# Attention projections in plain float32, one head on each half of the array's rows

## The chip, the cores and the metric

The kernel runs on one core of a Trainium2 chip. The number that counts is the device time of that core in microseconds (us), as the median over several executions. Beside the timed executions there is one profiled execution, whose trace records every instruction with its start, its duration and what it waited for. TensorE (PE) does the matrix products and the transposes, VectorE (DVE) and ScalarE (ACT) work on what PE leaves in PSUM, GpSimd (POOL) works on SBUF tiles only, and SyncE (SP) issues most transfers. PSUM has eight banks; a bank holds 512 float32 values in each of its 128 partitions.

## The reference

Attention without a softmax over the sequence (random features), and then a gated feed-forward layer without top-k or routing. B = H = 8, S = 576, D = 64, M = 128; 4608 tokens, d_model 512, d_ff 1536, all float32.

```python
def phi(x):                                   # x is q or k, scaled by 64 ** -0.25
    proj = np.einsum('bhsd,md->bhsm', x, omega)
    h = proj - np.sum(x * x, axis=-1, keepdims=True) / 2.0
    h = h - np.max(h, axis=-1, keepdims=True)
    return np.exp(h) / np.sqrt(m)

kv = np.einsum('bhsm,bhsd->bhmd', phi(k), v)
num = np.einsum('bhsm,bhmd->bhsd', phi(q), kv)
den = np.einsum('bhsm,bhm->bhs', phi(q), np.sum(phi(k), axis=2))[..., None] + 1e-06
x = num / den                                 # then all heads of a token side by side: 4608 x 512
out = (sigmoid(x @ w_gate) * (x @ w_val)) @ w_out
```

The change concerns the einsum for `proj`, for q and for k: 64 values of one head times a 64x128 matrix, for every token and head.

## The kernel before

**The stages.** A first stage, to about 531 us of the trace, does the attention and at the same time the first third of the gate and value products (`first_pass`, tile `gv`, line 246), chunk of tokens by chunk of tokens as the attention delivers them. Then the rest of the first pass is done while the last weights are converted. From 618 us on a second pass does the other products (`gated`, tile `gw`, line 350), and after it the output product (`last`, tile `po`, line 464). The last two are Strassen-like schemes in which every operand is split into a rounded part and a remainder, so that three products in the fast 32-bit type `fp32r` give float32 accuracy.

**The attention.** Two batch rows (1152 tokens, nine tiles of 128) form a unit u, of which there are four; p is a pair of heads, of which there are four; b is the half of the nine tiles that belongs to one batch row, the tile in the middle (number 4, `MID`) being shared. A task is one (u, p, b) of k or of q, or the squared norms of one (u, b). `projected` (line 508) is common to k and q. The tile `raw` holds the two heads of a pair one above the other: 64 rows of the partitions are head 0, 64 are head 1. `om_sb` has omega's transpose twice, in the upper left and the lower right block, and zeros elsewhere, so that one product with 128 rows gives 256 columns, 128 for each head.

For this product raw is split on ACT (`hi`, line 70) and POOL (`lo`, line 71), omega once in the same way, and each tile of tokens takes three `fp32r` products of 128x256 that add up (lines 546 to 548). `GROUPS` says which tiles of tokens share a bank: two tiles of both heads, that is 4 x 128 columns. DVE then takes the maximum over each 128 columns (`mx`, line 551), and joins it with the norm (`hm`, line 555).

For k (`keys`, line 560) DVE makes the bias `nb` (line 573), ACT the exponentials (line 586), one instruction for each tile and head, and PE the products with v (`pkv`, line 594), in plain float32. For q (`queries`, line 602) DVE makes `sub` (line 612) and `h` (line 614), PE transposes `h` (`pt`, line 625), ACT takes the exponential of a whole bank (`qp`, line 627), PE multiplies with kv (`pn`, line 637, plain float32), DVE divides (lines 642 to 648), PE transposes again (`px`, line 654), ACT copies (`xs`, line 660) and issues the transfer to `xT` in DRAM, from where `first_pass` loads it. The middle tile of q belongs to two batch rows: there line 637 issues two products, each with 64 of the 128 columns of the array.

**What sets the order.** Each engine works through its own list in a fixed order. The lists are made when the program is built: the generators of the tasks are advanced in turn (`attention`, up to six at a time), the attention by `RATE` steps for each half product of `first_pass`, and a scheduler then orders each engine's instructions by what is ready. Tiles come from pools with a fixed number of buffers (`RAWS`, `SPLITS`, `HS`, `XS` and so on); who wants a buffer waits until its last reader is done. Of the eight banks two belong to `gv` and six to the attention.

Of the kernel before, what the change touches and what calls it, by code (L numbers as in the profile page):

```python
# [9 lines left out]
F32 = mybir.dt.float32  # L10
# [17 lines left out]
GROUPS = {"k": (((0, 1), (2, 3), (4,)), ((5, 6), (7, 8))), "q": (((0, 1), (2, 3)), ((4,), (5, 6), (7, 8)))}  # L28
# [22 lines left out]
RATE = 14  # L51

RAWS, SPLITS, KPS, VS, HS, XS = 6, 5, 8, 3, 4, 3
# [46 lines left out]
def attn_glu_kernel(ctx: ExitStack, tc, qT, kT, qn, kn, va, om, ident, w, out):  # L100
# [411 lines left out]
    def projected(pool, name, u, p, b, src):  # L512
# [10 lines left out]

        groups = GROUPS[name][b]
        for some in (groups,) if name == "k" else [(g,) for g in groups]:
            parts = []
            for tiles in some:
                id_ = f"{name}{u}_{p}_{tiles[0]}"
                nt = len(tiles)
                hi, lo = (  # L530
                    pool.tile([P, 2 * P], F32R, tag=tag, bufs=SPLITS, name=f"{tag}{id_}")[:, : nt * P]
                    for tag in ("hi", "lo")
                )
                o = (tiles[0] - t0) * P
                split(nc, hi, lo, raw[:, o : o + nt * P], lo_engine=nc.gpsimd)
                parts.append((id_, tiles, hi, lo))
            yield None
            i0, i1 = some[0][0] - t0, some[-1][-1] + 1 - t0
            mx = pool.tile([P, MID + 1, 2], F32, tag="mx", bufs=4, name=f"mx{id_}")
            pps = []  # L540
            for id_, tiles, hi, lo in parts:
                pp = any_bank(f"pp{id_}")[:, : len(tiles) * 2 * M]
                for i, t in enumerate(tiles):
                    c = slice(i * P, (i + 1) * P)
                    o = pp[:, i * 2 * M : (i + 1) * 2 * M]
                    nc.tensor.matmul(o, lhsT=lo[:, c], rhs=omH, start=True, stop=False)
                    nc.tensor.matmul(o, lhsT=hi[:, c], rhs=omL, start=False, stop=False)
                    nc.tensor.matmul(o, lhsT=hi[:, c], rhs=omH, start=False, stop=True)
                pp = pp.rearrange("p (i m) -> p i m", m=M)
                m = mx[:, tiles[0] - t0 : tiles[-1] + 1 - t0]  # L550
                nc.vector.tensor_reduce(out=m.rearrange("p t h -> p (t h)"), in_=pp, axis=AX.X, op=ALU.max)  # L551
                pps.append((id_, tiles, pp))
# [7 lines left out]
    def keys(pool, u, p, b):  # L560
        kp = {}
        if b:
            kp[MID] = kmid.pop((u, p))
# [313 lines left out]
```

## Time and profile before

| | |
|---|---|
| median of 3 runs | 1262.45 us (1262.18 to 1266.67) |
| profiled execution, first to last instruction | 1265.4 us |
| mean granted TensorE clock in it | 0.954 |
| busy: PE, DVE, ACT, POOL | 1186.0, 876.1, 529.0, 542.9 us |
| attention (first transfer to last transpose) | 0 to about 531 us |
| rest of the first pass | 531 to 618 us |
| second pass and output product | 618 to 1265 us |

The page counts a matmul as busy from its start to the modelled end of its pipeline, so that matmuls overlap in the records: what one costs in a dense stretch is the distance from its start to the next one's. A plain float32 matmul stands in the trace as two records, each with a weight load of its own; an `fp32r` matmul and a transpose stand there as one. The row and column PEclk give the share of the full TensorE clock that was granted.

### The profile page before, as it was taken

The numbers are of one execution on the slowest core, as the hardware profiler recorded it, in microseconds if no ns is written. First come the engines' busy times: TensorE is split into PE (matmuls) and PEld (weight loads), VectorE is DVE, ScalarE is ACT, GpSimd is POOL, SyncE is SP. The second block draws the span as 40 slices with busy tenths as digits, with TensorE's granted clock in tenths as the row PEclk, the third lists the DMA queues.
The fourth block names the chain that finished last, engine by engine and source line by source line (L and its number), as shares of the span: only waits on it lengthen the run. The fifth ranks groups of instructions, "written<-read, shape, count | busy, mean of one in ns | idle before, by whom it ended". The sixth has DMA issues, their size and how long they took to land.

```text
span 1265.4 us, 23998 instructions
## 1 busy us (share of the span) xinstructions
PE 1186.0 (94%) x8828; PEld 1122.2 (89%) x8828; DVE 876.1 (69%) x1907; ACT 529.0 (42%) x1164; POOL 542.9 (43%) x599
## 2 busy tenths in 40 slices
PE   5789989999998999987999999999999899999998
PEld 5789878788977988865999999999998899999998
DVE  4788877999777565564666565665667777777773
ACT  5456755656344544322522222323234444343331
POOL 2454334755456232144176666666666311111110
PEclk7689879999889999998999999999999999999999
DMA  7557767776555331176423333233328676666662
GB/s 244 191 179 237 219 209 243 254 253 230 183 203 174 124 122 38 60 267 223 166 88 121 139 132 109 102 121 122 130 88 285 208 218 194 206 194 183 185 198 93
DMA packets 104950, 219.43 MB, mean 173 GB/s; under 512 B 11136, under 2 KB 42112, under 8 KB 103040
## 3 DMA queue, kind: packets, MB, share of 16 engines
q1 hardware_dynamic: 87984, 198.94, 47.5%
q10 hardware_dynamic: 16848, 18.95, 4.3%
q8 instruction: 70, 1.15, 0.4%
q14 instruction: 48, 0.39, 0.1%
HBM read 141.82 MB, written 76.02 MB: 172 GB/s over the span
## 4 chain that ended last, share of the span: by engine, by line
PE 66%; DVE 13%; DMA 7%; issue 6%; POOL 4%; ACT 2%; SPq 1%; ACTq 0%; DVEq 0%; POOLq 0%
PE gw L350 25%; PE po L464 20%; PE gv L246 6%; PE pkv L594 4%; PE pnq L637 4%; PE ptq L625 2%; DMA xT<-xsq 2%; DVE mxq L551 1%; DVE hq L614 1%; DMA u<-w 1%; DVE mxk L551 1%; DMA natk<-kn 1%; DVE hmq L555 1%; DMA rawk<-kT 1%; DVE u L215 1%
## 5 line engine op out<-in xcount | busy, mean ns | idle before, releaser
L350 PE MATMUL gw<-xl,u 128*128 128x256 f32 x3024 | 362.3, 282 | 4.2 <-DVE u L330 3.5
L350 PEld LDWEIGHTS gw<-xl,u 128*128 128x128 f32 x3024 | 361.1, 189 | 5.4 <-DVE u L330 4.3
L464 PE MATMUL po<-u,yh 128*128 128x256 f32 x1512 | 272.4, 283 | 0.0
L464 PEld LDWEIGHTS po<-u,yh 128*128 128x128 f32 x1512 | 234.7, 191 | 0.0
L464 PE MATMUL po<-u,yl 128*128 128x256 f32 x756 | 214.0, 283 | 4.0 <-DVE yl L71 4.0
L246 PE MATMUL gv<-xe,wh 128*128 128x512 f32 (+1 forms) x640 | 206.3, 397 | 1.6 <-POOL xe L71 1.4
L70 ACT ACTIVATE yh<-yr 128x896 fp32r<-128x896 f32 x108 | 100.2, 950 | 158.2 <-PE po L464 86.9
L464 PEld LDWEIGHTS po<-u,yl 128*128 128x128 f32 x756 | 144.2, 191 | 4.4 <-DVE yl L71 4.4
L246 PE MATMUL gv<-xe,wl 128*128 128x512 f32 (+1 forms) x320 | 128.1, 403 | 14.1 <-DVE ye L274 7.9
L246 PEld LDWEIGHTS gv<-xe,wh 128*128 128x128 f32 x640 | 119.6, 199 | 19.1 <-POOL xe L71 3.3
L71 POOL TENSOR_TENSOR yl<-yr,yh 128x896 fp32r<-128x896 f32 x17 | 37.9, 2228 | 216.0 <-PE po L464 139.9
L71 DVE TENSOR_TENSOR yl<-yr,yh 128x896 fp32r<-128x896 f32 x91 | 103.0, 1144 | 31.3 <-PE po L464 18.3
L330 DVE TENSOR_TENSOR u<-gw,p 128x256 f32<-128x256 f32 x144 | 60.7, 421 | 58.9 <-PE gw L350 50.5
L594 PEld LDWEIGHTS pkv<-v,kpk 128*128 128x128 f32 x512 | 82.3, 220 | 21.5 <-ACT kpk L586 18.5
L594 PE MATMUL pkv<-v,kpk 128*128 128x66 f32 x512 | 88.3, 301 | 12.9 <-ACT kpk L586 12.5
L71 POOL TENSOR_TENSOR lok<-rawk,hik 128x256 fp32r<-128x256 f32 (+1 forms) x80 | 54.4, 697 | 98.6 <-ACT hik L70 98.4
L71 POOL TENSOR_TENSOR loq<-rawq,hiq 128x256 fp32r<-128x256 f32 (+1 forms) x80 | 57.5, 727 | 81.0 <-ACT hiq L70 77.6
L246 PEld LDWEIGHTS gv<-xe,wl 128*128 128x128 f32 x320 | 63.3, 199 | 24.9 <-DVE ye L274 9.1
L455 DVE TENSOR_TENSOR yr<-yr 128x128 f32<-128x128 f32 x144 | 58.2, 437 | 38.9 <-DMA yr<-ye 38.4
L637 PEld LDWEIGHTS pnq<-kv,qpq 128*128 128x128 f32 (+1 forms) x640 | 73.0, 195 | 4.8 <-ACT qpq L627 2.8
L637 PE MATMUL pnq<-kv,qpq 128*128 128x66 f32 (+1 forms) x640 | 76.5, 279 | 0.7 <-ACT qpq L627 0.7
L586 ACT ACTIVATE kpk<-ppk,nb 128x128 f32<-128x128 f32 x256 | 69.7, 391 | 15.9 <-DVE nb L573 15.6
(116 smaller groups left out, 2171.7 us busy)
## 6 DMA issues: line engine op xcount, KB each, us to landing
yl<-yl SPq DMA_DIRECT2D x36, 896.0 KB, 3.9
yr<-yl SPq DMA_DIRECT2D x72, 448.0 KB, 3.6
xr<-xT SPq DMA_DIRECT2D x68, 256.0 KB, 4.4
c<-w SPq DMA_DIRECT2D x22, 512.0 KB, 5.4
w<-c SPq DMA_DIRECT2D x11, 1024.0 KB, 4.7
v<-va SPq DMA_DIRECT2D x32, 330.0 KB, 3.3
natk<-kn SPq DMA_DIRECT2D x36, 256.0 KB, 4.5
natq<-qn SPq DMA_DIRECT2D x36, 256.0 KB, 3.8
```

The lines of the kernel that those rows point to most:

```text
L70: nc.scalar.activation(out=hi, in_=x, func=AF.Copy)
L71: (lo_engine or nc.vector).tensor_tensor(out=lo, in0=x, in1=hi.bitcast(F32), op=ALU.subtract)
L246: nc.tensor.matmul(gv, lhsT=u[:, s], rhs=v, start=(m == 0), stop=(m == 3 * KC - 1))
L330: return nc.vector.tensor_tensor(out=o, in0=a, in1=b, op=ALU.add)
L350: nc.tensor.matmul(o, lhsT=u[:, k, s], rhs=v[:, kc, :], start=(first and m == 0), stop=(m == 5), skip_group_check=not first,)
L455: nc.vector.tensor_tensor(out=raw[:, o], in0=raw[:, a], in1=raw[:, b], op=op)
L464: nc.tensor.matmul(o, lhsT=u[:, i, :], rhs=v[:, k, :], start=(j + m == 0 and n in (1, 6, 5, 4)), stop=(j == NPAIR - 1 and m == 2), skip_gr ...
L551: nc.vector.tensor_reduce(out=m.rearrange("p t h -> p (t h)"), in_=pp, axis=AX.X, op=ALU.max)
L586: nc.scalar.activation(out=kp[t][:, h, :], in_=pp[:, 2 * i + h, :], func=AF.Exp, bias=nb[:, t - t0, h : h + 1], scale=SCALE,)
L594: nc.tensor.matmul(pkv[:, h, :], lhsT=kp[b * MID + i][:, h, :], rhs=v[:, i, h, :], start=(i == 0), stop=(i == MID),)
L625: nc.tensor.transpose(out=pt[:, i, :], in_=h_sb[:, i, :], identity=id_sb)
L637: nc.tensor.matmul(pn[r, 2 * i + h, :], lhsT=qp[:, 2 * i + h, r], rhs=kvs[u, p, bb][:, h, :], start=True, stop=True,)
```

## The change

The projections are done in plain float32 from `raw` and `om_sb` themselves: the copies `hi` and `lo`, their pools, and the split of omega go. For a group of several tiles (`by_head`) each head has a product of its own, on its own 64 rows of the array with omega's 64x128 block, and its own bank; the products of the two heads alternate. The groups have four tiles instead of two, so that a bank again holds 4 x 128 columns, now of one head. A middle tile that stands alone (`both_heads`) is one product with all 128 rows and 256 columns, as before, but in plain float32. What follows works by bank as it did, with `mx`, `hm` and `sub` for four tiles at once, and `x`, `px`, `xs` and the transfer to `xT` too. `RATE` goes from 14 to 12 and `HS` from 4 to 5.

```diff
-GROUPS = {"k": (((0, 1), (2, 3), (4,)), ((5, 6), (7, 8))), "q": (((0, 1), (2, 3)), ((4,), (5, 6), (7, 8)))}
+GROUPS = {"k": (((0, 1, 2, 3), (4,)), ((5, 6, 7, 8),)), "q": (((0, 1, 2, 3),), ((4,), (5, 6, 7, 8)))}
...
-RATE = 14
-
-RAWS, SPLITS, KPS, VS, HS, XS = 6, 5, 8, 3, 4, 3
+RATE = 12
+
+RAWS, KPS, VS, HS, XS = 6, 8, 3, 5, 3
...
-    omH = const.tile([P, 2 * M], F32R, name="omH")
-    omL = const.tile([P, 2 * M], F32R, name="omL")
-    split(nc, omH, omL, om_sb)
...
+        def by_head(tiles):
+
+            pps = [any_bank(f"pp{name}{u}_{p}_{tiles[0]}_{h}") for h in range(2)]
+            for i, t in enumerate(tiles):
+                for h in range(2):
+                    r = slice(h * D, (h + 1) * D)
+                    nc.tensor.matmul(
+                        pps[h][:, i * M : (i + 1) * M], lhsT=raw[r, (t - t0) * P : (t - t0 + 1) * P],
+                        rhs=om_sb[r, h * M : (h + 1) * M], start=True, stop=True, skip_group_check=True,
+                    )
+            return [(tiles, (h,), pp.rearrange("p (i m) -> p i m", m=M)) for h, pp in enumerate(pps)]
+
+        def both_heads(t):
+
+            pp = any_bank(f"pp{name}{u}_{p}_{t}")[:, : 2 * M]
+            nc.tensor.matmul(pp, lhsT=raw[:, (t - t0) * P : (t - t0 + 1) * P], rhs=om_sb, start=True, stop=True)
+            return [((t,), (0, 1), pp.rearrange("p (i m) -> p i m", m=M))]
+
...
-                split(nc, hi, lo, raw[:, o : o + nt * P], lo_engine=nc.gpsimd)
...
-                    nc.tensor.matmul(o, lhsT=lo[:, c], rhs=omH, start=True, stop=False)
-                    nc.tensor.matmul(o, lhsT=hi[:, c], rhs=omL, start=False, stop=False)
-                    nc.tensor.matmul(o, lhsT=hi[:, c], rhs=omH, start=False, stop=True)
...
+            for tiles in some:
+                for part in by_head(tiles) if len(tiles) > 1 else both_heads(tiles[0]):
+                    ts, hs, pp = part
+                    m = mx[:, ts[0] - t0 : ts[-1] + 1 - t0, hs[0] : hs[-1] + 1]
+                    m = m.rearrange("p t h -> p (t h)")
+                    nc.vector.tensor_reduce(out=m, in_=pp, axis=AX.X, op=ALU.max)
+                    pps.append(part)
...
+            x = pool.tile([P, nt, 2, D], F32, tag="x", bufs=XS, name=f"x{id_}")
+            parts = []
+            for ts, hs, pp in pps:
+                n = nt * len(hs)
+                h_sb = pool.tile([P, n, M], F32, tag="h", bufs=HS, name=f"h{id_}_{hs[0]}")
...
+            for hs, n, h_sb in parts:
+                pt = any_bank(f"pt{id_}_{hs[0]}")[:, : n * P].rearrange("p (i s) -> p i s", s=P)
...
+            for hs, n, qp in qps:
+                pn = any_bank(f"pn{id_}_{hs[0]}")[:, : n * E].rearrange("p (i e) -> p i e", e=E)
```

**Where instructions now stand.** Three places on PE's list show it. In the changed program line 527 is the product of one head (64 rows), 536 that of a middle tile, 592 is `pkv`, 243 is `gv`. In a name such as `ppk_3_0_1`, 3 is the pair, 0 the first tile of the group, and the last number the head.

Before, PE's list in the second unit: the end of a k projection with its middle tile, and what follows it.

```order
L548 MATMUL ppk_2_2_1949<-omH,hik_2_2_1908 128x256
L546 MATMUL ppk_2_4_1957<-omH,lok_2_4_1913 128x256
L547 MATMUL ppk_2_4_1957<-omL,hik_2_4_1912 128x256
L548 MATMUL ppk_2_4_1957<-omH,hik_2_4_1912 128x256
L637 MATMUL pnq_1_7_1981<-kv_1_1_1047,qpq_1_7_1921 128x66 x4
```

Every projection is a triple of 128x256, and all of them use all rows and columns of the array.

The changed program, PE's list in the same unit: the middle of a k projection, into which another pair's `pkv` is put.

```order
L527 MATMUL ppk_3_0_0_1771<-om_sb,rawk_3_0_1710 128x128
L592 MATMUL pkv_2_0_1720<-v_2_0_1676,kmid_2_4_0_1690 128x66
L592 MATMUL pkv_2_0_1720<-v_2_0_1676,kp_2_0_1_1685 128x66 x4
L592 MATMUL pkv_2_0_1720<-v_2_0_1676,kmid_2_4_0_1690 128x66
L527 MATMUL ppk_3_0_1_1772<-om_sb,rawk_3_0_1710 128x128
```

Products with 64 rows now stand next to products with 128, and a pair of heads can be torn apart by other work.

The changed program, a little further on, where a q projection meets the first pass.

```order
L243 MATMUL gv_0_0_1857<-xe_3_1854,wl_238 128x512
L527 MATMUL ppq_1_0_0_1900<-om_sb,rawq_1_0_1805 128x128
L243 MATMUL gv_0_0_1857<-xe_3_1854,wh_237 128x512 x2
L527 MATMUL ppq_1_0_1_1901<-om_sb,rawq_1_0_1805 128x128
L527 MATMUL ppq_1_0_0_1900<-om_sb,rawq_1_0_1805 128x128
```

Here a single product of 64 rows stands between two of the first pass. Over the whole list the 512 products of line 527 form 86 unbroken runs, 37 of them of eight products and 18 of a single one; before, the 288 tiles of tokens took 864 products, and now they take 512 of line 527 and 32 of line 536.

More of the change, by code (lines that the diff above doesn't have):

```diff
@@ L537, in projected @@
             yield None
             i0, i1 = some[0][0] - t0, some[-1][-1] + 1 - t0
-            mx = pool.tile([P, MID + 1, 2], F32, tag="mx", bufs=4, name=f"mx{id_}")
+            mx = pool.tile([P, MID + 1, 2], F32, tag="mx", bufs=4, name=f"mx{name}{u}_{p}_{some[0][0]}")
             pps = []
[L541 to L552, printed above, removed]
+            for tiles in some:
[5 more added lines that the diff above has]
+                    pps.append(part)
@@ L553, in projected @@
             s = sq[:, i0:i1, 2 * p : 2 * p + 2]
-            hm = pool.tile([P, MID + 1, 2], F32, tag="hm", bufs=4, name=f"hm{id_}")[:, i0:i1]
+            hm = pool.tile([P, MID + 1, 2], F32, tag="hm", bufs=4, name=f"hm{name}{u}_{p}_{some[0][0]}")[:, i0:i1]
             nc.vector.scalar_tensor_tensor(
@@ L594, in keys @@
                 nc.tensor.matmul(
[L595 removed]
+                    pkv[:, h, :], lhsT=kp[b * MID + i, h], rhs=v[:, i, h, :],
                     start=(i == 0), stop=(i == MID),
@@ L622, in queries @@
-            yield
-            pt = any_bank(f"pt{id_}")[:, : n * P].rearrange("p (i s) -> p i s", s=P)
-            for i in range(n):
-                nc.tensor.transpose(out=pt[:, i, :], in_=h_sb[:, i, :], identity=id_sb)
-            qp = pool.tile([P, n, P], F32, tag="qp", bufs=HS, name=f"qp{id_}")
-            nc.scalar.activation(out=qp, in_=pt, func=AF.Exp)
-            yield
-            pn = any_bank(f"pn{id_}")[:, : n * E].rearrange("p (i e) -> p i e", e=E)
-            for i, t in enumerate(tiles):
-                if t == MID:
-                    mine = ((0, slice(0, P // 2)), (1, slice(P // 2, P)))
-                else:
-                    mine = ((b, slice(0, P)),)
-                for h in range(2):
+            x = pool.tile([P, nt, 2, D], F32, tag="x", bufs=XS, name=f"x{id_}")
@@ new lines, in queries @@
+            yield
+            qps = []
+            for hs, n, h_sb in parts:
+                pt = any_bank(f"pt{id_}_{hs[0]}")[:, : n * P].rearrange("p (i s) -> p i s", s=P)
+                for i in range(n):
+                    nc.tensor.transpose(out=pt[:, i, :], in_=h_sb[:, i, :], identity=id_sb)
+                qp = pool.tile([P, n, P], F32, tag="qp", bufs=HS, name=f"qp{id_}_{hs[0]}")
+                nc.scalar.activation(out=qp, in_=pt, func=AF.Exp)
+                qps.append((hs, n, qp))
+                yield
```

94 lines of the change are left out of this document (44 added, 50 removed).

## Prediction

> **What bounds the kernel now.** I read the windows by stage first, since the change touches the attention alone.
>
> ```profile
> core 0: us, PE busy (x) PEld busy (x) DVE busy (x) ACT busy (x) POOL busy (x), PEclk, DMA share, GB/s
> 0.00:64.00 64.00, 44.62 (x208) 42.66 (x209) 38.30 (x82) 32.33 (x90) 23.06 (x32) 0.69 0.66 218
> 64.00:192.00 128.00, 113.70 (x818) 106.88 (x816) 106.13 (x273) 78.12 (x216) 56.97 (x67) 0.86 0.67 210
> 192.00:531.00 339.00, 318.48 (x2216) 280.82 (x2217) 253.30 (x645) 170.10 (x474) 149.70 (x178) 0.97 0.52 172
> 531.00:618.00 87.00, 74.70 (x301) 59.10 (x301) 48.28 (x69) 26.16 (x40) 37.48 (x32) 0.92 0.57 201
> 618.00:1265.40 647.40, 634.53 (x5290) 632.79 (x5288) 430.06 (x842) 222.33 (x345) 275.74 (x292) 1.00 0.48 159
> ```
>
> The last 647 us are not touched by the change. In the attention, from 192 us on, PE is busy for 318 of 339 us at a clock of 0.97: what PE is spared or given there is time. Before that the clock is lower and PE waits more. DVE is full in two stretches only:
>
> ```profile
> 64.00:160.00 96.00, 87.45 (x674) 83.59 (x673) 83.30 (x216) 60.17 (x167) 45.46 (x53) 0.91 0.68 213
> 224.00:320.00 96.00, 90.88 (x632) 78.64 (x630) 90.79 (x208) 57.00 (x161) 58.58 (x67) 0.99 0.72 239
> ```
>
> That is 87% and 95%, in 192 of the attention's 531 us. Then the waits of PE up to 531 us (us in total, times, longest):
>
> ```profile
> PE pkv L594 <- ACT kpk L586: 12.5, 12, 2.8
> PE ppk L546 <- POOL lok L71: 10.3, 2, 8.8
> PE ppq L546 <- POOL loq L71: 0.9, 1, 0.9
> ```
>
> The split of q and k, for all its 112 us on POOL, makes PE wait 11.2 us, and 8.8 of these are the program's start, where the first transfer is on its way till 7.5. So the change is to be judged mainly by what the projections cost PE.
>
> **The projections on PE.** There are 144 records in each of six groups like the first and last here, 864 in all:
>
> ```profile
> L546 PE MATMUL ppk<-omH,lok 128*128 128x256 f32 x144 | 46.9, 325 | 11.2 <-POOL lok L71 10.3 <-ACT qpq L627 0.9
> ...
> L547 PE MATMUL ppq<-omL,hiq 128*128 128x256 f32 x144 | 41.9, 291 | 0.0
> ```
>
> These durations overlap; the cost is the step between starts. First and last of 18 in a row, and the next thing:
>
> ```profile
> 440.55 0.28 PE L546 MATMUL ppq<-omH,loq 128*128 128x256 f32 x1
> ...
> 442.54 0.28 PE L548 MATMUL ppq<-omH,hiq 128*128 128x256 f32 x1
> 442.66 0.27 PE L625 MATMUL ptq<-id_sb,hq 128*128 128x128 f32 x1
> ```
>
> (442.66 - 440.55) / 18 = 0.117 us, so 864 x 0.117 = 101 us at the full clock.
>
> What a plain float32 product costs is shown by `pnq`, two records each, on the whole array and, for the middle tile, on halves of its columns:
>
> ```profile
> 449.61 1.90 PE L637 MATMUL pnq<-kv,qpq 128*128 128x66 f32 x16
> 451.35 0.49 PE L654 MATMUL pxq<-id_sb,xq 128*128 128x128 f32 x3
> ...
> 246.08 0.69 PE L637 MATMUL pnq<-kv,qpq 128*64 128x66 f32 x16
> 246.70 0.39 PE L546 MATMUL ppq<-omH,loq 128*128 128x256 f32 x1
> ...
> 247.04 0.28 PE L548 MATMUL ppq<-omH,hiq 128*128 128x256 f32 x1
> 247.25 0.45 PE L637 MATMUL pnq<-kv,qpq 128*64 128x66 f32 x8
> 247.63 0.50 PE L246 MATMUL gv<-xe,wl 128*128 128x512 f32 x1
> 247.97 0.62 PE L246 MATMUL gv<-xe,wh 128*128 128x512 f32 x2
> 248.43 0.39 PE L246 MATMUL gv<-xe,wl 128*128 128x512 f32 x1
> ```
>
> On the whole array a record takes 1.74 / 16 = 0.109 us. On column halves 16 records take 0.62 and 8 take 0.38, so a further record costs (0.62 - 0.38) / 8 = 0.030: a half-sized weight load would explain 0.055, and the rest is that two halves work at once. But each such run has a price at its ends. From the `ppq` before it to the second `gv` behind it there are 247.97 - 247.04 = 0.93 us; in a dense stretch these steps would be 0.117 + 8 x 0.030 + 0.23 (0.46 for two `gv`, last rows) = 0.59. So a change between whole array and halves and back costs 0.34 us.
>
> No row shows halves of rows. Take it that they behave as halves of columns do. A record has 128 weight columns, so 0.109, and two records of different heads go together. Following PE's new list run by run, with alternating heads paired, the 512 products take 286 places of two records: 286 x 2 x 0.109 = 62 us. There are 86 runs; a run's first weight load is twice that of the rows above, 0.05 more, so 86 x 0.39 = 34 us. The 32 middle tiles are two records of 128x256: at least what fp32r takes, 0.23, at most what two fp32r records of 128x512 take, 0.46; since the column halves pass 66 columns in up to 0.06 us, which makes 0.23 for 256, I take the upper end, 15 us. Together 111 against 101: **PE is given 10 us**. The bounds: with nothing for the ends of runs -24; with no pairing and no ends 512 x 2 x 0.109 + 15 = 127, +26; with both prices +59.
>
> The Trainium skill says under "Key Properties" of "TensorEngine Tiling (Array Packing)" that tiles run independently of one another, but that a change of the tiling mode drains TensorE. The trace agrees for column halves, with the 0.34 us above; for row halves no run here shows it. "TensorE: Matmul & The Clock Gate", Part 3, "Measured speedup vs the span model", gives 3.07 for four row tiles; an estimate from that page, 1.53 for two, would put the 512 products at 112 / 1.53 = 73 us instead of 62, and the result 11 us higher.
>
> **What else goes.**
>
> ```profile
> L71 POOL TENSOR_TENSOR lok<-rawk,hik 128x256 fp32r<-128x256 f32 (+1 forms) x80 | 54.4, 697 | 98.6 <-ACT hik L70 98.4
> L71 POOL TENSOR_TENSOR loq<-rawq,hiq 128x256 fp32r<-128x256 f32 (+1 forms) x80 | 57.5, 727 | 81.0 <-ACT hiq L70 77.6 <-PE ppq L546 2.7 <-DMA rawk<-kT 0.5
> L70 ACT ACTIVATE hik<-rawk 128x256 fp32r<-128x256 f32 (+1 forms) x80 | 30.2, 392 | 20.1 <-PE ppk L548 9.2 <-PE ppq L548 8.3 <-POOL lok L71 1.5
> L555 DVE SCALAR_TENSOR_TENSOR hmq<-mxq,sqq 128x4 f32<-128x4 f32 x64 | 19.1, 312 | 0.0
> L612 DVE TENSOR_TENSOR subq<-sqq,hmq 128x4 f32<-128x4 f32 x64 | 17.6, 288 | 0.1
> L85 DVE TENSOR_SCALAR c<-c 128x512 uint32<-128x512 uint32 x22 | 13.2, 602 | 0.1
> 556.07 0.42 DVE L85 TENSOR_SCALAR late<-late 128x512 uint32<-128x512 uint32 x1
> ```
>
> PE's waits for the split: 1.3 at the start (8.8 less 7.5), 1.5 and 0.9 later, **-4** (bounds 0 and -11). On DVE 32 of the 64 `hm` and 32 of the `sub` go, 32 x (0.312 + 0.288) = 19 us; DVE sets the pace in 192 of 531 us, that is 7, and since PE is nearly full in the same stretches I count half, **-4** (0 and -19). The weight conversion's short DVE steps take 0.60 on average where one takes 0.42 undisturbed, and POOL, which shares the load, does half as much of it: some 22 x 4 steps at up to 0.18, half of 16, in a third of the time on the path, **-2**. On ACT 61 us of copies go, with 80 waits for `hi` buffers in front of the exponentials; ACT is busy for half its time, so of the 12.5 us in which `pkv` waits for exponentials I take **-2** (0 and -12).
>
> On the other side, q is delivered in groups of 512 tokens, and the first product of the first pass, which needs 256, has to wait for twice the work of a group: at most a few us at the start, while PE does other tasks: 0 to +3, I take 0. `raw` is now held until the product has read it, and a q group holds two banks of six instead of one: no PE wait of the list above is for a bank by name, and I count nothing; if pairs of banks came late, `pt` and `pn` would queue behind on PE. The bigger `xT` transfers and `xs` copies are half in number, off the path.
>
> The sum: +10 - 4 - 4 - 2 - 2 = -2. The profiled execution, 1265.4 us, lies 3 above the median of the runs, 1262.45, from which the change is counted: **1260 us**.
>
> **Rivals.**
>
> *Halves pair and the ends cost little* (the changes often fall on places where PE waits anyway, or row halves need no change-over). Projections 77, PE -24. Where DVE is 87 to 95% busy only DVE's relief counts, some 9 us of its 25; in the other 64% of the time PE's 24 count in full, 15; with the waits, 6, that is -30: **1232**. For it: the 0.34 is measured on column halves. Against it: all changes in the trace cost about that, after `gv` as after `ppq`.
>
> *The halves do not pair, slower.* If a product of 64 rows holds the whole array as one of 128 does, PE gets +26, and less the 12 us of relief this is +14: **1276**; with the ends paid too, +47: **1309**. It decides early: with the ends paid, the sum is over 0.5% slower as soon as a pair of records takes 0.124 us instead of 0.109 (572 x 0.015 is the 8.3 us between -2 and +6.3). For it: plain float32 needs two records for each product, in list order, and nothing here shows two records of different rows at once. Against it: the column halves.
>
> *The clock, slower.* Plain float32 does not always count as work for the clock:
>
> ```profile
> 20.40:23.80 3.40, 3.40 (x18) 3.40 (x18) 0.98 (x2) 3.26 (x11) 0.00 (x0) 0.50 1.02 380
> 30.60:34.05 3.45, 3.45 (x19) 3.45 (x18) 3.21 (x6) 1.25 (x3) 2.71 (x4) 0.50 0.91 325
> 34.05:37.40 3.35, 1.32 (x11) 1.12 (x10) 3.35 (x7) 2.63 (x7) 3.35 (x5) 1.00 0.89 320
> 320.80:324.20 3.40, 3.40 (x17) 3.40 (x18) 1.72 (x8) 0.00 (x0) 1.78 (x2) 0.50 0.24 99
> ```
>
> Under nothing but `pkv` (first row) and `pnq` (last row) a full PE stays at half clock, and after a stretch of fp32r projections (second row) it is granted 1.00 (third). If the new projections count like `pnq`, the clock falls back: 0.69 in the first 64 us is full clock for 38% of them, 24 us, in which PE is busy for 70%, so up to 17 us of work double; a later dip like that at 320 doubles some 5 us more each: +10 to +25 on the sum, at +17 **1277**. Against it: 128 columns keep the array twice as busy as 66.
>
> **How the numbers follow.** Halves pair with the ends paid 0.50, pair with cheap ends 0.22, do not pair 0.19, clock 0.09. The likeliest gives 1260, and 1245 to 1275 by the bounds of its terms. The range, 1230 to 1302, takes in the second case but its lowest part, the clock, and the unpaired case but its upper end. Runs of this kernel tell about 0.5%, 6 us, from no change: of the likeliest case a third lies below 1256, half within, a sixth above 1269. Faster: 0.50 x 0.34 + 0.22, which is 0.39; the same: 0.25; slower: the rest, 0.36.
>
> **What would show it.** Right: in a run of eight products the 16 records start in eight pairs, 0.109 us from pair to pair, so that the run takes some 0.9 us, and 0.3 to 0.4 us more are lost where it begins and ends; the attention ending near 530. Records of line 527 at 0.109 one by one show the unpaired case; a dense step at the ends of runs the cheap one; PEclk below 0.69 before 64 us the clock. The forecast is wrong if the attention ends more than 10 us from 531 with PE's projections as I cost them: then a bank, a buffer or the order decides, which I count at nothing.

## The result, and the profile after

The kernel before took 1264.12 us (median of 11 executions, 1258.41 to 1272.14) on the chip where the two were compared, the changed one 1268.96 us (11, 1264.26 to 1277.18). The ratio is **1.0063, with an interval of 1.0038 to 1.0088**: slower by 8 us, where -2 was forecast. The two medians lie only 4.8 us apart; the ratio is that of the fast executions alone and stands for 8 us, and the repeat below has 7.7 us between its medians.

One execution of a kernel can lie 1% from another, and the two that were profiled show it: the changed kernel's span is 1263.4 us, at the lower edge of its times, against 1265.4 us before. So the 8 us are not in the difference of these two pages. What the pages show is which work and which waits changed; what a part costs is read from ratios over several executions. The clock of the profiled execution before, 0.954, is also lower than usual: 82 executions of that kernel beside the experiments below have 0.966 on average.

The stages of the changed kernel (columns as in the windows shown of before):

```profile
0.00:64.00 64.00, 50.48 (x271) 43.42 (x272) 35.85 (x83) 26.17 (x67) 7.99 (x10) 0.84 0.68 223
64.00:192.00 128.00, 114.09 (x813) 102.56 (x811) 100.56 (x246) 65.08 (x169) 37.05 (x35) 0.83 0.64 204
192.00:531.00 339.00, 320.32 (x2399) 271.87 (x2399) 228.87 (x609) 136.43 (x353) 74.94 (x73) 0.97 0.53 177
531.00:618.00 87.00, 74.32 (x321) 59.41 (x321) 50.41 (x69) 26.28 (x41) 34.88 (x30) 0.94 0.56 198
```

DVE (third pair of numbers), ACT and POOL have clearly less to do; POOL's 150 us from 192 us on became 75. PE did not become less busy, and its clock did not rise. (The 0.84 of the first row flatters it: the view counts full clock until the first clock event of the trace, here at 32 us, while the records till then have the step of the half clock; 0.84 - 0.25 = 0.59 is nearer. Where the first event comes at 10 to 14 us, as in the kernels before and with full rows, the row is too high by about 0.1.) In the two stretches where DVE was full, it no longer is, with 79% and 78%:

```profile
64.00:160.00 96.00, 84.81 (x623) 77.15 (x622) 75.48 (x191) 47.07 (x119) 21.38 (x19) 0.83 0.61 193
224.00:320.00 96.00, 86.90 (x639) 72.28 (x640) 75.21 (x186) 40.79 (x113) 33.20 (x34) 0.95 0.68 230
```

PE's waits up to 535 us:

```profile
PE pt L631 <- DVE h L617: 18.2, 16, 3.8
PE pkv L592 <- ACT kp L582: 13.8, 12, 2.3
PE ppk L527 <- DMA rawk<-kT: 5.6, 2, 4.6
PE pn L644 <- DVE h L617: 3.1, 1, 3.1
```

The wait for the split, 10.3 us, is gone; what is left at that place is the first transfer, 5.6. The wait of the transposes for `h` is 18.2 us, where it was 11.6 and 5.0.

One run of eight products at the full clock, between two groups of transposes:

```profile
201.78 1.03 PE L631 MATMUL pt<-id_sb,h 128*128 128x128 f32 x8
202.74 1.16 PE L527 MATMUL ppq<-om_sb,rawq 64*128 64x128 f32 x16
203.84 1.09 PE L631 MATMUL pt<-id_sb,h 128*128 128x128 f32 x8
204.77 1.00 PE L644 MATMUL pn<-kv,qp 128*128 128x66 f32 x8
```

The 16 records start in eight pairs (7 ns apart within a pair), and from the second pair on the step is 0.111 us: the halves do pair. The run begins 0.96 us after the first transpose, where 8 x 0.109 = 0.87 would be dense (+0.09), lasts 1.10 where 8 x 0.111 = 0.89 would do (+0.21), and the eight transposes behind it take 0.93 instead of 0.87 (+0.06): **0.36 us for the two ends of a run**.

### The profile page after: what moved, and what is told of

Same layout as the page of the kernel before. It is cut to its first block, busy times and chain, and to the rows that moved or that the text cites. A ratio compares the mean times of both kernels' runs of the same rounds, so it can differ in the third digit from the quotient of the medians.

```text
span 1263.4 us, 23711 instructions
## 1 busy us (share of the span) xinstructions
PE 1189.8 (94%) x9052; PEld 1105.9 (88%) x9052; DVE 848.5 (67%) x1842; ACT 474.5 (38%) x971; POOL 431.3 (34%) x439
## 4 chain that ended last, share of the span: by engine, by line
PE 68%; DVE 11%; DMA 7%; issue 7%; POOL 4%; ACT 2%; SPq 1%; ACTq 0%; DVEq 0%; POOLq 0%
PE gw L347 25%; PE po L461 20%; PE gv L243 7%; PE pkv L592 6%; PE pn L644 4%; PE ppk L527 2%; PE pt L631 2%; POOL xe L71 2%; DMA xr<-xT 2%; PE ppq L527 1%; DVE mxk L550 1%; DMA u<-w 1%; DVE mxq L550 1%; DMA xT<-xs 1%; DVE h L617 1%
## 5 line engine op out<-in xcount | busy, mean ns | idle before, releaser
L243 PE MATMUL gv<-xe,wh 128*128 128x512 f32 (+1 forms) x640 | 200.0, 392 | 2.9 <-POOL xe L71 2.8
L243 PE MATMUL gv<-xe,wl 128*128 128x512 f32 (+1 forms) x320 | 128.3, 403 | 13.2 <-DVE ye L271 10.3
L71 POOL TENSOR_TENSOR xe<-xr,xe 128x512 fp32r<-128x512 f32 (+1 forms) x40 | 49.5, 1251 | 172.7 <-ACT xe L70 164.8
L592 PE MATMUL pkv<-v,kp 128*128 128x66 f32 x512 | 88.4, 308 | 13.9 <-ACT kp L582 13.8
L592 PEld LDWEIGHTS pkv<-v,kp 128*128 128x128 f32 x512 | 80.4, 222 | 22.6 <-ACT kp L582 19.2
L96 POOL TENSOR_TENSOR c<-c 128x512 f32<-128x512 f32 x22 | 28.2, 1283 | 165.5 <-DVE c L94 91.0
L452 DVE TENSOR_TENSOR yr<-yr 128x128 f32<-128x128 f32 x144 | 64.4, 482 | 28.1 <-DMA yr<-ye 27.5
L644 PE MATMUL pn<-kv,qp 128*128 128x66 f32 (+1 forms) x640 | 75.5, 273 | 3.1 <-DVE h L617 3.1
L644 PEld LDWEIGHTS pn<-kv,qp 128*128 128x128 f32 (+1 forms) x640 | 70.4, 189 | 8.2 <-DVE h L617 3.5
L633 ACT ACTIVATE qp<-pt 128x512 f32<-128x512 f32 (+1 forms) x80 | 43.6, 555 | 89.1 <-PE pt L631 85.9
```

The source lines that it names most:

```text
L71: (lo_engine or nc.vector).tensor_tensor(out=lo, in0=x, in1=hi.bitcast(F32), op=ALU.subtract)
L96: nc.gpsimd.tensor_tensor(out=x, in0=x, in1=r, op=ALU.add)
L243: nc.tensor.matmul(gv, lhsT=u[:, s], rhs=v, start=(m == 0), stop=(m == 3 * KC - 1))
L452: nc.vector.tensor_tensor(out=raw[:, o], in0=raw[:, a], in1=raw[:, b], op=op)
L592: nc.tensor.matmul(pkv[:, h, :], lhsT=kp[b * MID + i, h], rhs=v[:, i, h, :], start=(i == 0), stop=(i == MID),)
L633: nc.scalar.activation(out=qp, in_=pt, func=AF.Exp)
```

## The experiments

All ratios are to the kernel before, on the same chip, with their 95% intervals. A difference between two of these ratios is good to some 0.4%, 5 us. Except where a line says otherwise, the kernels compute what the reference wants.

**The changed kernel once more**, with the next three on one chip.

> The changed kernel once more, for a second trace and a tighter ratio. Theory 1 (the projections cost PE some 10 us more, as predicted, and the relief of 12 us that I put against it is not there): ratio to before 1.005 to 1.009. Theory 2 (the relief is there, but the later first gate and the bigger groups cost as much or more): the same ratio. Theory 3 (the clock decides from run to run): the ratio moves by more than 0.4% from 1.0063, and the low-clock time before 530 us differs from the first trace's by over 20 us.

Measured: 1.0064 (1.0038 to 1.0091). The result stands.

**Full rows instead of halves.** Each head's product reads all 128 rows; the other head's rows meet the zero block of omega. Banks, groups, order and RATE are those of the changed kernel.

```diff
-  pps[h][:, i*M:(i+1)*M], lhsT=raw[r, ...], rhs=om_sb[r, h*M:(h+1)*M],
+  pps[h][:, i*M:(i+1)*M], lhsT=raw[:, ...], rhs=om_sb[:, h*M:(h+1)*M],
```

> The changed kernel with each head's product on all 128 rows (omega's block with its zeros), same banks, groups and order; only the array's mode differs. No two products run at once, and no run has ends. On PE: 512 x 2 x 0.109 = 112 us instead of 62 + 86 x 0.34 = 91, that is +20 us (the middle tiles stay). Theory 1 (PE sets the pace in the attention): 10 to 20 us slower than the changed kernel, 1.014 to 1.022 against before. If PE's work in the projections is mostly hidden behind DVE (theory 2): under 6 us slower, 1.006 to 1.011.

Measured: **0.9944 (0.9913 to 0.9975)**, 1251.7 us. I had expected slower. It beats both kernels, so the halves cost 15 us, and all the rest of the change gains 7. Its stages:

```profile
0.00:64.00 64.00, 45.42 (x282) 43.55 (x283) 40.47 (x96) 27.23 (x70) 8.72 (x11) 0.82 0.69 229
64.00:192.00 128.00, 115.32 (x852) 107.71 (x851) 103.26 (x250) 66.42 (x171) 37.22 (x35) 0.92 0.69 222
192.00:531.00 339.00, 331.33 (x2403) 297.37 (x2401) 233.37 (x605) 141.54 (x360) 81.14 (x77) 1.00 0.54 182
```

PE is busier than in the changed kernel (331 against 320 us in the third row), and its clock is higher in the second row (0.92 against 0.83) and the third (1.00 against 0.97).

**Runs kept whole.** The eight products of a group stand together in the order (64 runs instead of 86, 262 places instead of 286).

```diff
-                    nc.tensor.matmul(
+                    pin(nc.tensor.matmul(
```

> The changed kernel with the eight products of a group kept together in PE's list: 64 runs instead of 86, 262 places of two records instead of 286. On PE: 22 x 0.34 + 24 x 0.218 = 13 us less. Theory 1: 8 to 13 us faster than the changed kernel, 0.996 to 1.000 against before. Theory 2: within 4 us of the changed kernel, 1.003 to 1.007.

Measured: 1.0021 (0.9991 to 1.0051), 4 to 5 us less than the changed kernel, at the edge of what the intervals tell apart. That is a third of the 14 us that 22 x 0.39 and 24 places of 0.218 would give. The clock may be a part of why: it is 0.949 on average over the executions here, 0.956 in the changed kernel beside it, and in the trace the half clock adds 58 us to PE's work in the attention, where it adds 46 and 52 in the changed kernel (the table further down).

**The split put back as work that nobody reads**, copies on ACT and subtractions on POOL, in fewer buffers than before.

```diff
+  hi, lo = (pool.tile([P, 2 * P], F32R, tag=tag, bufs=(2 if tag == "hi" else 1), ...) for tag in ("hi", "lo"))
+  split(nc, hi, lo, raw[:, o : o + len(two) * P], lo_engine=nc.gpsimd)
```

> The changed kernel with the removed split put back as work that nobody reads: 160 copies on ACT and 160 subtractions on POOL, in the old sizes and places, so that only their load on the two engines and on SBUF returns. Theory 1 (their removal relieved nothing that PE waits for): within 4 us of the changed kernel, 1.003 to 1.009. Theory 2 (the predicted relief by ACT, POOL and the undisturbed DVE is real): 5 to 12 us slower than the changed kernel, 1.010 to 1.016.

Measured: 1.0362 (1.0323 to 1.0401), 38 us above the changed kernel, far more than expected. With two `hi` buffers ACT waits for POOL here, so the size can't be put down to load alone; two runs below put POOL's and ACT's half back one by one.

**The ends of runs by themselves.** The kernel with full rows, and ahead of each of the 64 groups one product of 64 rows and 4 columns.

```diff
+            nc.tensor.matmul(
+                pps[0][:, :4], lhsT=raw[:D, (tiles[0] - t0) * P : (tiles[0] - t0 + 1) * P],
+                rhs=om_sb[:D, :4], start=True, stop=True, skip_group_check=True,
+            )
```

> The kernel whose products use all 128 rows (0.9944 against before), with one tiny product of 64 rows and 4 columns put before each of the 64 groups and overwritten by them: PE changes to halves and back 64 times, but nothing is computed on halves. Price on PE: 64 x (0.34 + two short records, 0.1) = 28 us. Theory A (the ends of runs make the change slow; PE's time counts in full): 20 to 28 us slower than without, 1.010 to 1.017 against before, low-clock time in the attention within 15 us of the 55 us without. Theory B (what makes it slow is the clock, which falls because half the rows are at work; a drained PE has slack elsewhere): under 12 us slower than without, below 1.004.

Measured: 1.0101 (1.0061 to 1.0140), 1272.8 us. That is 0.0157 above the full rows, 20 us for 64 changes, **0.31 us each**, the tiny product's own time included. What a change takes on PE's list in this kernel:

```profile
410.12 0.60 PE L664 MATMUL px<-id_sb,x 128*128 128x128 f32 x4
410.65 0.38 PE L524 MATMUL ppq<-om_sb,rawq 64*128 64x4 f32 x2
410.96 2.05 PE L530 MATMUL ppq<-om_sb,rawq 128*128 128x128 f32 x16
412.85 0.60 PE L664 MATMUL px<-id_sb,x 128*128 128x128 f32 x4
```

The tiny product starts 0.53 us after the four transposes, where 4 x 0.109 = 0.44 would be dense (+0.09), takes 0.31, and the 16 records behind it 1.89, where they take 1.79 in the kernel with full rows (+0.10): 0.50 us, or 32 for 64. So some two thirds of what the ends take on PE are paid in time.

**Pairing taken away.** Head 0's four products, then head 1's (442 places instead of 286).

```diff
-            for i, t in enumerate(tiles):
-                for h in range(2):
+            for h in range(2):
+                for i, t in enumerate(tiles):
```

> The changed kernel with the four products of head 0 in a row and then those of head 1, so that two products rarely run at once (442 places of two records in the list instead of 286); ends of runs as before (83). PE's work: 156 x 0.218 = 34 us more than in the changed kernel. Theory A (PE's time counts in full): 25 to 34 us slower than the changed kernel, 1.026 to 1.034. Theory B (the clock): the halves leave the clock low whether paired or not, and the longer projections fill what were waits: 5 to 20 us slower, 1.010 to 1.022, with at least the changed kernel's 117 us of low clock in the attention, though PE has more to do. Should more work on halves raise the clock, theory B falls.

Measured: 1.0110 (1.0066 to 1.0154). PE has (442 - 286) x 0.22 = 34 us more to do, and the kernel is 6 us slower than the changed one. So the pairing, which works, hardly pays.

**Only the split removed.** The kernel before with plain float32 products of 128x256, still in groups of two tiles, RATE 14.

```diff
-  nc.tensor.matmul(o, lhsT=lo[:, c], rhs=omH, start=True, stop=False)
-  nc.tensor.matmul(o, lhsT=hi[:, c], rhs=omL, start=False, stop=False)
-  nc.tensor.matmul(o, lhsT=hi[:, c], rhs=omH, start=False, stop=True)
+  nc.tensor.matmul(o, lhsT=raw[:, (t - t0) * P : (t - t0 + 1) * P], rhs=om_sb, start=True, stop=True)
```

> The kernel before with one part of the change alone: no split, each tile's product of 128 rows and 256 columns in plain float32; groups of two tiles, RATE 14 and everything else as before. PE's work: 288 x 2 x 0.22 = 127 instead of 101, 26 us more. If the split's removal is what gives the 0.6% of the full-row kernel: 0.992 to 0.998. If the groups of four tiles by head (half as many small steps on DVE, half as many transfers) give it: 1.005 to 1.015, since PE's work is then not paid for.

Measured: 0.9980 (0.9950 to 1.0010). PE's projections take 288 x 2 x 0.222 = 128 us instead of 101 and the kernel is no slower. If PE's work counts in full, as the run with two of three products below shows for the kernel before, going without the split is worth some 27 + 2.5 = 30 us, not the 8 that I counted for it (4 for waits, 2 and 2 for POOL and ACT). This run also changes the kind of product, from fp32r to plain float32, and no run separates the two. Its stages show a higher clock:

```profile
0.00:64.00 64.00, 48.22 (x248) 41.12 (x248) 41.61 (x108) 31.10 (x80) 11.77 (x14) 0.89 0.70 233
64.00:192.00 128.00, 114.95 (x750) 103.90 (x751) 104.72 (x275) 69.18 (x180) 33.07 (x31) 0.92 0.71 233
```

The clock was 0.69 and 0.86 here before, and is 0.89 and 0.92. (Over the executions it is 0.966 before and 0.975 here, a smaller step than between these two traces.)

**POOL's half of the split put back** on the changed kernel: 160 subtractions that nobody reads and that need only `raw`.

```diff
+  lo = pool.tile([P, 2 * P], F32R, tag="lo", bufs=1, ...)
+  nc.gpsimd.tensor_tensor(out=lo, in0=x, in1=x, op=ALU.subtract)
```

> The changed kernel with the old POOL work alone put back as work nobody reads: 160 subtractions on raw, in the old sizes, waiting for no engine and waited for only by the next use of raw's buffer. If POOL's load on SBUF disturbs DVE enough to matter: 4 to 12 us slower than the changed kernel, 1.009 to 1.016. If the 38 us that the split's return cost came from ACT and POOL waiting for each other: within 4 us, 1.003 to 1.009.

Measured: 1.0180 (1.0145 to 1.0215), 15 us above the changed kernel. Three views of its attention, the first two of groups by line and the third of PE's waits:

```profile
L546 POOL TENSOR_TENSOR lok<-rawk 128x256 fp32r<-128x256 f32 (+1 forms) x80 | 50.1, 626 | 82.0 <-DMA rawk<-kT 78.1
L546 POOL TENSOR_TENSOR loq<-rawq 128x256 fp32r<-128x256 f32 (+1 forms) x80 | 47.8, 597 | 76.7 <-DMA rawq<-qT 72.3
L560 DVE SCALAR_TENSOR_TENSOR hmq<-mxq,sqq 128x8 f32<-128x8 f32 (+1 forms) x47 | 11.7, 250 | 0.2
L81 DVE TENSOR_SCALAR c<-c 128x512 f32<-128x512 f32 x22 | 12.7, 579 | 0.2
PE gv L243 <- POOL wl L71: 6.1, 1, 6.1
PE gv L243 <- POOL xe L71: 4.1, 5, 2.5
```

The same two DVE groups in the changed kernel:

```profile
L554 DVE SCALAR_TENSOR_TENSOR hmq<-mxq,sqq 128x8 f32<-128x8 f32 (+1 forms) x48 | 10.0, 209 | 0.2
L81 DVE TENSOR_SCALAR c<-c 128x512 f32<-128x512 f32 x22 | 10.0, 452 | 0.2
```

98 us of POOL work that nobody reads cost 15 us, and the trace shows three things that they may act through. DVE's small steps and half of the weight conversion's get slower (0.250 against 0.209 us and 0.579 against 0.452 in the groups shown), the long steps do not; DVE is busy for 9 us more in all (857.7 against 848.5 and 849.1). The weights and activations that POOL prepares for the gate come later, since they queue on POOL behind subtractions that wait for `raw` (78 and 72 us of such waits): PE waits 6.1 and 4.1 us for them, against 0.4 and 2.8 in the changed kernel. And the half clock adds 62 us to PE's work, against 46 and 52. How the 15 us divide among the three isn't shown. PE's list of waits before, which is where I had looked for the split's price, shows none of the three as the split's.

**ACT's half of the split put back**: 160 copies that nobody reads, in one buffer.

```diff
+  hi = pool.tile([P, 2 * P], F32R, tag="hi", bufs=1, ...)
+  nc.scalar.activation(out=hi, in_=x, func=AF.Copy)
```

> The changed kernel with the 160 copies of q and k on ACT put back, unread, in one buffer, without POOL's part and so without waits between the two. By the prediction's term (2 us, bounds 0 and 12): 1.006 to 1.010. If load on ACT costs what load on POOL did (14 us for 112 us of work, so 8 for ACT's 61): 1.011 to 1.015.

Measured: 1.0039 (1.0008 to 1.0069), no slower than the changed kernel. ACT's part alone costs nothing that the runs can tell, POOL's alone 15 us; the other 23 of the 38 us come only with both together, and what they consist of stays open.

**RATE back to 14** on the kernel with full rows.

```diff
-RATE = 12
+RATE = 14
```

> Full rows for each head, and RATE set back from 12 to 14, so that fewer gate products (583 by the order against 641) come before the attention's end. It is the part of the change that is only a number, alone, on the fastest kernel so far (0.994). If the attention is limited by DVE and the waits, fewer gate products in it leave PE idle there and their time comes behind it: 0.996 to 1.002. If it is limited by PE, the number only moves work from one place to another: within 0.003 of 0.994.

Measured: 0.9964 (0.9932 to 0.9996), 2.5 us above the same kernel with 12; the intervals overlap. Against the kernel with only the split removed (0.9980), this one has groups of four and a bank for each head: 2 us less, within the intervals of either.

**TensorE spared work in the kernel before.** One of the three fp32r products is left out, so the projection is less exact; all else stays.

```diff
-  nc.tensor.matmul(o, lhsT=hi[:, c], rhs=omL, start=False, stop=False)
```

> The kernel before without one of its three fp32r products per tile, that of hi with the low part of omega: the projection is then less exact, and everything else (the split, the order, the banks) is as before. PE is spared 288 x 0.117 = 34 us of dense work and nothing else. By the prediction's step that what PE is spared is time: 0.973 to 0.978. If, as the run with head 0's four products ahead of head 1's suggests (34 us more of PE's work for 6 us), PE's work is only partly time here: 0.988 to 0.998.

Measured: **0.9710 (0.9666 to 0.9753)**, 36 us for 34 us of PE's work.

**TensorE spared work in the new order, without halves.** Full rows, each product three times the same bfloat16 product of the upper halves of the numbers, which makes the features less exact.

```diff
-  nc.tensor.matmul(pps[h][...], lhsT=raw[...], rhs=om_sb[...], ...)
+  for _ in range(3):
+      nc.tensor.matmul(pps[h][...], lhsT=upper(raw[...]), rhs=upper(om_sb[...]), ...)
```

> Full rows for each head, but each product is three times the same bfloat16 product of the numbers' upper halves, so the features are less exact; order, banks and groups as in the full-row kernel (0.994). By the step of the fp32r products, 0.117 for 256 columns, TensorE's work in the projections falls from 127 to some 95 us if a bfloat16 record takes as long, 30 us less, about what pairing spares less its ends. If time spared for TensorE is time in this order too, and the halves' own ends and clock take back what pairing spares: 0.965 to 0.975. If in this order waits for DVE and ACT take the place of TensorE's work: 0.986 to 0.996.

Measured: 0.9744 (0.9702 to 0.9787). The step of a record, and that of the plain float32 record with full rows, from the timelines of the two kernels:

```profile
403.99 3.22 PE L532 MATMUL ppq<-om_sb,rawq 128*128 128x128 bf16 x52
```

```profile
194.91 1.95 PE L526 MATMUL ppq<-om_sb,rawq 128*128 128x128 f32 x16
196.70 1.04 PE L630 MATMUL pt<-id_sb,h 128*128 128x128 f32 x8
```

Less the 0.22 us that the last one takes by itself, (3.22 - 0.22) / 51 = 0.059 us, three of them 0.176; the plain product takes (196.70 - 194.91) / 8 = 0.224. So 512 x 0.048 = 24 us are spared, and a few more on the middle tiles, and the kernel is 0.0200 x 1260 = 25 us faster than with full rows. **Time spared for PE is time, in the new order too.** What takes the pairing's gain away belongs to the halves.

**Halves only later, and only at the start.** Full rows in the first 12 groups (the first 104 us) and halves in the other 52; then the complement.

```diff
+            halved[0] += 1
...
-                    r = slice(h * D, (h + 1) * D)
+                    r = slice(h * D, (h + 1) * D) if halved[0] > 12 else slice(0, P)
```

> The first 12 of the 64 groups (in the changed kernel these lie in the first 104 us) multiply over all 128 rows, with omega's zero block, the other 52 on halves. All 64 on full rows gave 0.994, all on halves 1.006. If the halves lose mainly at the start, where the clock of the changed kernel stays low until 32 us and that of the full rows rises at 10, most of the 15 us come back: 0.994 to 0.999. If they lose at the ends of runs wherever these lie, only 12/64 of it comes back, 3 us: 1.002 to 1.006.

> The complement of the kernel with full rows in its first 12 groups (1.000): halves in these 12 alone, full rows in the other 52. If the loss is the sum of a part at the start (8 us) and a part later (7 us): 0.998 to 1.003. If a loss at the start is made up for later by work that is waiting anyway: 0.993 to 0.997.

Measured: 0.9999 (0.9968 to 1.0030) and 0.9968 (0.9940 to 0.9997). Against the full rows' 0.9944 the 52 later groups cost 7 us and the 12 first 3 (not told from 0), against 15 for all 64; with some 5 us of doubt on each these agree with a sum. Neither place holds the whole loss.

## Where the halves' gain went

The start of the attention shows how low the clock can stay. PE's timeline in the changed kernel:

```profile
7.64 2.08 PE L527 MATMUL ppk<-om_sb,rawk 64*128 64x128 f32 x16 [1.04 <-DMA rawk<-kT]
9.65 1.22 PE L536 MATMUL ppk<-om_sb,rawk 128*128 128x256 f32 x2
10.80 2.07 PE L527 MATMUL ppk<-om_sb,rawk 64*128 64x128 f32 x8
...
29.45 2.08 PE L527 MATMUL ppk<-om_sb,rawk 64*128 64x128 f32 x16
```

With full rows, the same list:

```profile
7.07 3.57 PE L526 MATMUL ppk<-om_sb,rawk 128*128 128x128 f32 x16 [0.69 <-DMA rawk<-kT]
10.47 0.60 PE L535 MATMUL ppk<-om_sb,rawk 128*128 128x256 f32 x2
10.91 1.05 PE L526 MATMUL ppk<-om_sb,rawk 128*128 128x128 f32 x8
```

With pairing taken away, at the start and at two later places:

```profile
7.43 3.10 PE L527 MATMUL ppk<-om_sb,rawk 64*128 64x128 f32 x16 [1.14 <-DMA rawk<-kT]
10.46 1.22 PE L536 MATMUL ppk<-om_sb,rawk 128*128 128x256 f32 x2
...
61.82 3.10 PE L527 MATMUL ppq<-om_sb,rawq 64*128 64x128 f32 x16
...
66.74 3.10 PE L527 MATMUL ppq<-om_sb,rawq 64*128 64x128 f32 x16
```

A middle tile takes 0.60 us at the full clock and 1.22 at half. The first clock event of a trace is the change to full clock; the records ahead of it have the step of the half clock. In these three traces it comes at 10.3 us with full rows, at 32.1 in the changed kernel and at 78.3 without pairing. But the kind of product alone does not set this moment. The six traces that begin with full rows and have no split have it at 10.2 to 12.9 us. Of the eight that begin with halves five have it at 31.9 to 78.3, and three at 10.2 to 11.7. One of these three is the kernel with POOL's work put back, whose PE list is that of the changed kernel for the first 1985 records:

```profile
7.01 2.08 PE L527 MATMUL ppk<-om_sb,rawk 64*128 64x128 f32 x16 [0.50 <-DMA rawk<-kT]
9.02 1.22 PE L536 MATMUL ppk<-om_sb,rawk 128*128 128x256 f32 x2
10.17 1.30 PE L527 MATMUL ppk<-om_sb,rawk 64*128 64x128 f32 x8
```

Its first event comes at 10.5 us. So PE on halves can get the full clock as early as on full rows, and often does not; why, no run shows. What does differ from kind to kind is how long the half clock lasts. With full rows PE goes back to half from 17.1 to 30.8, where `pkv` is most of its work, and in the windows from 32 to 48 us the clock is 0.89 with full rows, 0.61 in the changed kernel:

```profile
32.00:48.00 16.00, 9.59 (x80) 9.00 (x78) 13.24 (x30) 9.73 (x29) 3.44 (x4) 0.89 0.81 272
```

```profile
32.00:48.00 16.00, 15.02 (x74) 13.27 (x72) 8.43 (x21) 8.23 (x26) 1.26 (x1) 0.61 0.70 230
```

PE is busy for 15 of the 16 us there in the changed kernel, for 9.6 with full rows: so it is not a lack of work in PE's list that keeps the clock down there.

For the whole attention I added up PE's records until the last `px`: each at its step in a dense stretch at full clock (a half product as if it were always paired), then what the granted clock of 0.5 adds to those that started under it; the rest of the time is ends, unpaired halves and waits. All in us, from one trace each; the row of the changed kernel has both of its traces.

| kernel | to the last `px` | PE's work | half clock adds | rest |
|---|---|---|---|---|
| before | 532 | 412 | 48 | 72 |
| only the split removed | 528 | 439 | 31 | 58 |
| full rows | 508 | 431 | 23 | 54 |
| full rows, ends added | 534 | 438 | 34 | 62 |
| full rows, then halves | 520 | 385 | 43 | 92 |
| changed | 522, 525 | 375 | 46, 52 | 102, 98 |
| changed, runs kept whole | 527 | 375 | 58 | 94 |
| changed, ACT's work back | 521 | 375 | 44 | 102 |
| changed, not paired | 532 | 374 | 43 | 116 |
| changed, POOL's work back | 548 | 375 | 62 | 111 |

(The changed kernels and those with full rows have 641 gate products in this time, the unpaired one 636, the first two rows 670 and 672, at 0.23 us each, or 0.117 for the 192 of them that have 256 columns.)

From full rows to halves PE's work falls by 56, and the time rises by 14 in the traces, 15 by the ratios. The half clock adds 23 more. Of the 48 more in the rest, 60 products that find no partner take 30 places more than as pairs, 30 x 0.22 = 7, the ends of 86 runs 86 x 0.36 = 31, and some 10 are left for waits. Three of PE's waits with full rows are below those of the changed kernel, by 1.4, 6.7 and 1.6 us, while those for the gate's operands are some 3 above:

```profile
PE pkv L591 <- ACT kp L581: 12.4, 10, 4.5
PE pt L630 <- DVE h L616: 11.5, 8, 5.3
...
PE pn L643 <- DVE h L616: 1.5, 1, 1.5
```

So -56 + 7 + 31 + 23 + 10 = +15 (by the changed kernel's second trace -56 + 7 + 31 + 29 + 6 = +17). That halves lower the clock is shown: PE's list has the same order in both kernels, and they differ in nothing but the rows that the products use; over many executions the clock is 0.973 with full rows (12) and 0.955 with halves (23), which counts as full the time ahead of the first event, 32 us in the two traces with halves. (Without pairing the same average is 0.977, but there the first event comes at 78 us, and with the time ahead of it the half clock lasts 116 us until the last `px`.) That the lower clock costs these 23 us is worked out from the records, not tried by itself. Executions of one kernel bear it out in part: among the 12 with full rows, each us more at half clock goes with 0.30 us more of time (standard error 0.05). Until the last `px` the half clock, with the time ahead of the first clock event, lasts 55 us with full rows and 117 in the changed kernel, and 62 x 0.30 is 19. What in the halves lowers the clock stays open. That the ends alone do it is not shown: with 64 tiny products the half clock adds 11 us more in the one trace, but over the executions the clock is 0.973 with them (6) and without, and in the first 64 us (0.81 against 0.82 with full rows) they change nothing:

```profile
0.00:64.00 64.00, 49.10 (x288) 46.07 (x288) 37.67 (x91) 26.47 (x68) 8.03 (x10) 0.81 0.67 223
64.00:192.00 128.00, 119.69 (x834) 113.61 (x834) 94.62 (x238) 65.61 (x169) 34.52 (x33) 0.85 0.65 205
```

Why the unpaired halves, with 34 us more of work, cost only 6 us more is in part in the table: the half clock adds 3 to 9 less, and of the rest's 116 some 41 are unpaired places and 30 ends, so that waits are some 15 us shorter. PE comes later to the transposes, which then wait less for `h` (9.0 us, where it was 18.2).

## Why the prediction was wrong

**What bounds the kernel: right where no halves are.** "What PE is spared or given there is time" holds with 36 us for 34 in the kernel before and 25 for 24 in the new order. Between paired and unpaired halves it does not: 34 us of work, 6 us of time.

**PE's work in the projections: right, term by term.** Pairing at 0.109 (0.111 measured), ends at 0.39 (0.36 by the rows; 0.31 as time, with the tiny product), the middle tiles at 0.46 (0.44 by their dense step): the 111 us are in the trace. The rival in which halves do not pair and the one with cheap ends both fell: the step between pairs is 0.111 us, and 64 changes cost 20 us.

The Trainium skill says in "TensorEngine Tiling (Array Packing)", "Key Properties", that changing the tiling mode drains TensorE; the 0.36 us of row halves agree, beside the 0.34 of column halves.

**The step that failed: that PE is given 10 us.** It turns 111 - 101 us of work into time at an unchanged clock, and has halves cheaper than full rows by 127 - 111 = 16 us. Measured, halves are 15 us dearer. The two ways agree on PE's work (-56 + 7 + 31 = -18), and differ by the 23 us of half clock and 10 of waits, for which the sum had no term. I had the clock as a rival at 0.09, asking whether it would fall below the level of before. The traces' half clock, 48 us before and 46 and 52 after, says that it did not, but the trace before had a low clock for its kernel. Over the executions the clock is 0.966 before and 0.955 after, which is 27 us more at half clock: it did fall, as the rival said. The sum came out 10 us short, the lower end of the rival's +10 to +25, though no run shows that the clock alone makes these 10. (Its 24 us of full clock in the first 64 were too many: the 0.69 counts the 13.6 us ahead of the first clock event as full, and the full clock lasted 10 us there.) What the sum needed was the clock that the change without halves would have had, where the half clock adds 23. The clock belonged into the sum of the likeliest case, as a term for each kind of product.

**The second step that failed: what the split's removal is worth.** I counted 4 + 2 + 2, and some 30 come out of the runs, the change from fp32r to plain float32 included. By the table, the half clock's share of this is 48 - 31 = 17, and the rest became 14 shorter; by the clocks of the executions (0.966 and 0.975, 22 us at half clock, where these two traces lie 43 apart) its share is nearer to 9. I had looked at PE's own waits for the split (11.2 us, 8.8 of them at the start) and priced POOL at 2 us for slowing DVE; POOL's part alone, put back on the changed kernel, costs 15. ACT's term, 2, was nothing that the runs can tell.

The terms by the runs, taken apart at the kernels between, in us of 1260:

| part | counted | measured |
|---|---|---|
| PE's plain float32 with full rows, 288 x 2 x 0.222 against 101 | +26 | +27 (PE's work) |
| split removed | -8 | -30 (-2.5 less the 27 above) |
| groups of four, a bank for each head | -4 | -2 (not told from 0) |
| RATE 12 | 0 | -2 (not told from 0) |
| halves instead of full rows | -16 | +15 |
| sum | -2 | +8 |

Two errors of 22 and 31 us in opposite directions left 10 in the sum. That the time, 1269, lies in the range is luck: the two errors nearly cancel. The sign was the other one.

**The later first gate** was taken as 0 to 3 us. The first `gv` starts at 67.9 us before, at 77.6 and 80.4 in the changed kernel, at 73.6 with full rows (77.2 with RATE 14) and at 55.8 where only the split is gone: so groups of four do put it off, by more than I said. What that costs by itself wasn't tried; it lies within the -2 of the groups.

**DVE's relief** was to count in the stretches where DVE is full. It fell from 87% and 95% to 79% and 78% there, and nothing was gained that the runs can tell from 0.

**What would show it.** The pairs, the 0.111 and the 0.36 came as described, and the attention ended 7 to 10 us earlier than in the profiled execution before, short of the bound at which I would have called the costing wrong. That sign could not work: the profiled execution before was itself 3 us above its median, the first one after 4 below, and the clock differs from one execution to the next.

## What to carry to other kernels

Before giving a product half of the array's rows, try the same product on all rows with zeros in the other half: here that is 15 us faster, beats both kernels, and leaves every other part of the change in place. Price a kind of matmul by its step, by the ends of its runs and by the clock that goes with it, over several executions, since one trace's clock can mislead; and compare with the other ways to do the same change, not only with the kernel before. Work on an engine that nobody waits for is not free: look at what queues behind it and whom it slows, or put it back alone and time it.

## What was not expected of the hardware

Plain float32 products on 64 rows go with a lower clock than the same products on 128 rows in the same order: 0.955 against 0.973 over 23 and 12 executions, and 117 and 131 us of half clock against 55 in the attention. The moment of the first full clock is no sign of it: after the same PE list on halves it came at 10.5 us in one trace and at 32.1 in another. The Trainium skill says in "TensorE: Matmul & The Clock Gate", Part 1, that one busy window of about 3.4 us releases the clock; here 15 busy us of 16 came at a clock of 0.61, so a busy PE alone was not enough.

98 us of POOL subtractions that nobody reads cost 15 us, while the 160 copies put back on ACT cost nothing that the runs can tell.
